# The first load of a residual add, issued as two half-loads from two queues

## The chip, the cores and the metric

The kernel runs on one core of one Trainium2 chip. The metric is the device time of one execution in microseconds; the time before is the median of three runs. Profiles come from a single profiled execution, so times inside the kernel are read against that execution and not against the median.

## The reference

```python
B, S, D = 512, 32, 640
x, fx: normal * 0.05, shape (512, 32, 640), bfloat16;  alpha: one bfloat16
def reference(x, fx, alpha):
    return x + alpha * fx
```

Each of x, fx and the output holds 10,485,760 bf16 values, 20.97 MB. The kernel must read two of them and write one: 62.92 MB in all, with one multiplication and one addition for each value.

## The kernel before, in words

All three tensors are seen as 128 partitions by 81,920 values, and a partition's row is counted in units of 512 values (1 KiB), of which it has 160. One SBUF tile `t` holds 207.5 units in each partition: units 0 to 160 are for x, and become the output in place; the rest is room for fx. Parts of fx that come late are put where x has not been loaded yet, or over fx parts that are used up.

The order of the work is written out by hand in the string `PLAN`, one step on a line, and the schedule is manual: each engine and queue gets its instructions in the order of the plan, and waits only where the data demand it. The steps are:

- `f a b p` loads units a to b of fx to place p of the tile (line 101, `load_f`). `x a b` loads x in place (line 97, `load_x`).
- `a` loads alpha (line 105), copied to 8 partitions of a small tile. DVE fills a row of ones (line 107), the matmul of line 109 spreads alpha over 128 partitions, and DVE copies it out of PSUM (line 111).
- `m a b` multiplies the fx part by alpha on DVE (line 114). `c a b` adds it to x on DVE (line 117).
- `s a b` stores units a to b (line 120). Of the three stores the first is held back until the multiplication of units 112.5 to 134.5 is done.

Every DMA of the kernel before is issued from SP (`nc.sync`): eleven large ones and the small one of alpha. Each large one has 128 rows, one a partition, of 8 to 64 KiB; consecutive rows lie 160 KiB apart in device memory. The plan begins:

```
f 0 8 95
a
f 8 65 103
x 0 64
x 64 95
f 65 112.5 160
m 0 8
m 8 65
c 0 8
```

The first step, `f 0 8 95`, is the smallest of the large loads: 128 rows of 8 KiB, 1 MiB in all. The first six loads wait for nothing; the later ones wait for DVE to have used the room that they overwrite. The ScalarE engine (ACT) has no work in this kernel. A completion counter stands behind every DMA; there are eight of them (DMAHW0 to DMAHW7 in the built program), given out in the order of issue, and a DMA that gets a used counter waits for the one that had it before. At the end a nop on SP (line 132) waits for all but the last store.

Of the kernel before, what the change touches and what calls it, by code (L numbers as in the profile page):

```python
# [1 line left out]

# [4 lines left out]

ALU = mybir.AluOpType
F32 = mybir.dt.float32

P = 128
K = 512
ROW = 160
SPARE = 47.5

LANES = 8

PLAN = """
f 0 8 95
a
f 8 65 103  # L30
x 0 64
# [5 lines that stand above are left out]
c 8 64  # L37
c 64 65
x 95 112.5
x 112.5 160  # L40
m 65 95
c 65 95
f 112.5 142.5 160
m 95 112.5
c 95 112.5
f 142.5 160 190
m 112.5 134.5
s 0 64 | m 112.5 134.5
m 134.5 142.5
c 112.5 142.5  # L50
m 142.5 160
c 142.5 160
s 64 128
s 128 160
"""


@with_exitstack
def kernel(
    ctx: ExitStack,  # L60
    tc: tile.TileContext,
    x: bass.AP,
    fx: bass.AP,
    alpha: bass.AP,
    out: bass.AP,
):
    nc = tc.nc
    xv, fv, ov = (
        t.flatten_outer_dims().rearrange("(p n) d -> p (n d)", p=P) for t in (x, fx, out)
    )  # L70
    assert xv.shape[1] == ROW * K

    consts = ctx.enter_context(tc.tile_pool(name="consts", bufs=1))
    psum = ctx.enter_context(tc.tile_pool(name="psum", bufs=1, space=bass.MemoryType.PSUM))
    flat = ctx.enter_context(tc.tile_pool(name="flat", bufs=1))
    ctx.enter_context(tc.manual_schedule())
    t = flat.tile([P, int((ROW + SPARE) * K)], x.dtype, name="t")
    info = mybir.DependencyInfo(mybir.DependencyClass.Sync, mybir.DependencyReason.DATA)

    lanes = {}  # L80
    lies = []
    done = []

    def at(a, b):
        return t[:, int(a * K) : int(b * K)]

    def of(v, a, b):
        return v[:, int(a * K) : int(b * K)]

    def place(a, b):  # L90
        for c, d, p in reversed(lies):
            if c <= a and b <= d:
                return at(p + a - c, p + b - c)
        raise ValueError(f"fx {a} to {b} lies nowhere in one piece")

    def load_x(a, b):
        done.append(nc.sync.dma_start(out=at(a, b), in_=of(xv, a, b)))

    def load_f(a, b, p):
        lies.append((a, b, p))  # L100
        done.append(nc.sync.dma_start(out=at(p, p + b - a), in_=of(fv, a, b)))  # L101

    def load_alpha():
        a_n = consts.tile([LANES, 1], alpha.dtype, name="a_n")
        done.append(nc.sync.dma_start(out=a_n[:], in_=alpha[None, :].to_broadcast([LANES, 1])))  # L105
        ones = consts.tile([1, P], alpha.dtype, name="ones")
        nc.vector.memset(ones[:], 1.0)  # L107
        a_ps = psum.tile([P, 1], F32, name="a_ps")
        done.append(nc.tensor.matmul(a_ps[:], ones[:], a_n[0:1, :], start=True, stop=True))  # L109
        lanes["a"] = consts.tile([P, 1], F32, name="a_f")  # L110
        nc.vector.tensor_copy(out=lanes["a"][:], in_=a_ps[:])  # L111

    def multiply(a, b):
        done.append(nc.vector.tensor_scalar_mul(place(a, b), place(a, b), lanes["a"][:]))  # L114

    def add(a, b):
        done.append(nc.vector.tensor_add(at(a, b), at(a, b), place(a, b)))  # L117

    def store(a, b):
        done.append(nc.sync.dma_start(out=of(ov, a, b), in_=at(a, b)))  # L120

    does = {"x": load_x, "f": load_f, "a": load_alpha, "m": multiply, "c": add, "s": store}
    begun = {}
    for step in filter(None, PLAN.split("\n")):
        step, *later = step.split(" | ")
        what, *numbers = step.split()
        does[what](*map(float, numbers))
        begun[step] = done[-1]
        for other in later:
            tc.add_manual_dep(done[-1].ins, begun[other].ins.name, info, reason="begins late")  # L130

    rest = nc.sync.nop(nofuse=True)
    for i in done[:-1]:
        tc.add_manual_dep(rest.ins, i.ins.name, info, reason="all but the last store")


# [1 line left out]
_INS = ['x', 'fx', 'alpha']  # L138
_OUTS = [((512, 32, 640), 'bfloat16')]


# [23 lines left out]
```

## Time and profile before

| | |
|---|---|
| median of 3 runs | 151.05 us (151.03 to 151.10) |
| profiled execution | 151.06 us |
| span in that execution, first to last instruction | 149.3 us |
| VectorE (DVE) busy | 66.5 us, 45% of the span, 16 instructions |
| DMA queue q1 | 1744 packets, 62.92 MB, 98.1% of 16 engines' span |
| mean rate over the span | 421 GB/s |

The span is what the views of the profile cover; 151.06 us less 149.3 us leaves some 1.8 us that lie around it. DMA engines, of which the core has 16, are shown by their mean busy share and by the rate of what they moved. In the table of stretches the bytes of a packet are credited to one moment, so a short stretch can show more than the engines can move, and its neighbour less. "Issue to landing" is the time from the instruction that issues a DMA to its completion. DVE is VectorE, PE is TensorE, SPq is the queue of SyncE.

### The profile page before, as it was taken

To read this page: it belongs to the slowest core of one execution; us is meant where nothing else is said; L and a number is where in the kernel's file an instruction comes from. 1 tells how busy PE (TensorE), PEld (TensorE's weight loads), DVE (VectorE), ACT (ScalarE), POOL (GpSimd) and SP (SyncE) were. 2 spreads that over 40 slices of the span, in tenths; PEclk is the share of its full clock that TensorE was granted. 3 is DMA by queue.
4 is the path that set the end of the run, shared out by engine and by line. 5 is a ranking of instruction groups with operands and counts; after the bars stand their busy time and mean duration, and the time that the engine had idled before them with its cause. 6 is when DMAs were issued, how large, how long until landed. Compare 5 with 4: busy or idle time off the path is not lost.

```text
span 149.3 us, 85 instructions
## 1 busy us (share of the span) xinstructions
PE 0.2 (0%) x1; PEld 0.1 (0%) x1; DVE 66.5 (45%) x16; POOL 0.2 (0%) x4
## 2 busy tenths in 40 slices
PE   0000000000000000000000000000000000000000
PEld 0000000000000000000000000000000000000000
DVE  0300008920069999029999900599997000000000
POOL 0000000000000000000000000000000000000000
DMA  5969998969699999999999799899896969697994
GB/s 149 617 266 500 500 461 351 562 281 562 281 408 442 447 417 443 456 388 565 430 417 417 340 461 461 379 516 457 386 562 281 562 281 562 281 562 334 430 439 202
DMA packets 1745, 62.92 MB, mean 421 GB/s; under 512 B 209, under 2 KB 209, under 8 KB 209
## 3 DMA queue, kind: packets, MB, share of 16 engines
q1 hardware_dynamic: 1744, 62.92, 98.1%
q14 instruction: 1, 0.00, 0.0%
HBM read 41.94 MB, written 20.97 MB: 421 GB/s over the span
## 4 chain that ended last, share of the span: by engine, by line
DMA 38%; DVE 31%; another core or an unknown queue 4%; issue 2%; SPq 1%; DVEq 0%
DMA t<-in_x_dram 27%; DVE t L117 26%; DMA t<-in_fx_dram 11%; DVE t L114 5%; SPq L101 0%; SPq L105 0%; DVEq L117 0%
## 5 line engine op out<-in xcount | busy, mean ns | idle before, releaser
L117 DVE TENSOR_TENSOR t<-t 128x15360 bf16<-128x15360 bf16 (+4 forms) x7 | 43.6, 6251 | 11.7 <-DMA t<-in_x_dram 11.6
L114 DVE TENSOR_SCALAR t<-t,a_f 128x4096 bf16<-128x4096 bf16 (+4 forms) x7 | 22.8, 3265 | 30.7 <-DMA t<-in_fx_dram 30.7
L111 DVE COPY a_f<-a_ps 128x1 f32<-128x1 f32 x1 | 0.2, 158 | 5.0 <-PE a_ps L109 5.0
L107 DVE MEMSET ones<- 1x128 bf16 x1 | 0.2, 165 | 0.8 <-PEq L149 0.8
L109 PE MATMUL a_ps<-a_n,ones 1*128 1x1 bf16 x1 | 0.2, 158 | 5.8 <-DMA a_n<-in_alpha_dram 5.8
L149 POOL MEMSET const-bfloat16-1.0<- 128x1 bf16 x1 | 0.1, 101 | 0.0
L149 POOL MEMSET const-uint8-127<- 128x1 uint8 x1 | 0.1, 101 | 0.0
L109 PEld LDWEIGHTS <-ones 1*128 1x128 bf16 x1 | 0.1, 99 | 1.0 <-DVE ones L107 1.0
L149 POOL MEMSET const-float32-0.0<- 128x1 f32 x1 | 0.1, 98 | 0.2 <-issue 0.2
L149 POOL MEMSET const-float32-1.0<- 128x1 f32 x1 | 0.1, 98 | 0.0
## 6 DMA issues: line engine op xcount, KB each, us to landing
t<-in_fx_dram SPq DMA_DIRECT2D x1, 7296.0 KB, 21.3
t<-in_fx_dram SPq DMA_DIRECT2D x1, 6080.0 KB, 63.0
t<-in_x_dram SPq DMA_DIRECT2D x1, 6080.0 KB, 25.7
out_dram<-t SPq DMA_DIRECT2D x1, 4096.0 KB, 33.7
t<-in_x_dram SPq DMA_DIRECT2D x1, 3968.0 KB, 49.2
t<-in_fx_dram SPq DMA_DIRECT2D x1, 3840.0 KB, 16.4
t<-in_x_dram SPq DMA_DIRECT2D x1, 2240.0 KB, 11.7
t<-in_fx_dram SPq DMA_DIRECT2D x1, 2240.0 KB
```

What stands on the lines that cost most here:

```text
L107: nc.vector.memset(ones[:], 1.0)
L109: done.append(nc.tensor.matmul(a_ps[:], ones[:], a_n[0:1, :], start=True, stop=True))
L111: nc.vector.tensor_copy(out=lanes["a"][:], in_=a_ps[:])
L114: done.append(nc.vector.tensor_scalar_mul(place(a, b), place(a, b), lanes["a"][:]))
L117: done.append(nc.vector.tensor_add(at(a, b), at(a, b), place(a, b)))
L149: nc = _bacc.Bacc("TRN2", target_bir_lowering=False, num_devices=1)
```

## The change

The step `f 0 8 95` becomes `g 0 8 95`. A new function issues the same load as two DMAs: partitions 0 to 63 from SP, as before the first thing in its queue, and partitions 64 to 127 from ACT. Both halves have 64 rows of 8 KiB with the same source and destination addresses as before. The other steps, their order and their queues are untouched.

```diff
 PLAN = """
-f 0 8 95
+g 0 8 95
 a
 f 8 65 103
...
+    def load_f_halves(a, b, p):
+        lies.append((a, b, p))
+        for queue, rows in ((nc.sync, slice(0, P // 2)), (nc.scalar, slice(P // 2, P))):
+            done.append(queue.dma_start(out=at(p, p + b - a)[rows, :], in_=of(fv, a, b)[rows, :]))
+
...
-    does = {"x": load_x, "f": load_f, "a": load_alpha, "m": multiply, "c": add, "s": store}
+    does = {"x": load_x, "f": load_f, "g": load_f_halves, "a": load_alpha, "m": multiply, "c": add, "s": store}
```

In the built program the instructions of PE, DVE and GpSimd (POOL) stay as they were, SP issues as many DMAs as before, and ACT issues one. Since there is one DMA more, each completion counter from alpha's on moves up by one place.

## The prediction

> **What bounds the kernel now.** I read the page's totals first, then the table of stretches, then the timelines of SP and DVE, then the DMA issues. A change of 0.2%, 0.3 us, is about the least that a measurement of this kernel can tell from none.
>
> The totals, from the page:
>
> ```profile
> PE 0.2 (0%) x1; PEld 0.1 (0%) x1; DVE 66.5 (45%) x16; POOL 0.2 (0%) x4
> q1 hardware_dynamic: 1744, 62.92, 98.1%
> ```
>
> DVE is busy for 45% of the span, the 16 DMA engines for 98.1% of theirs. Whether the missing 2% lie in gaps or at the ends is told by the table of stretches (DVE's busy time fourth, DMA share and GB/s last):
>
> ```profile
> 0.00:1.70 1.70, 0.00 (x0) 0.10 (x1) 0.17 (x1) 0.20 (x4) 1.00 0.00 0
> 1.70:2.10 0.40, 0.00 (x0) 0.00 (x0) 0.00 (x0) 0.00 (x0) 1.00 2.14 348
> 2.10:2.70 0.60, 0.00 (x0) 0.00 (x0) 0.00 (x0) 0.00 (x0) 1.00 0.43 109
> 2.70:3.30 0.60, 0.00 (x0) 0.00 (x0) 0.00 (x0) 0.00 (x0) 1.00 0.87 300
> 3.30:4.70 1.40, 0.00 (x0) 0.00 (x0) 0.00 (x0) 0.00 (x0) 1.00 1.01 421
> ...
> 100.00:120.00 20.00, 0.00 (x0) 0.00 (x0) 14.74 (x3) 0.00 (x0) 1.00 0.97 419
> 120.00:140.00 20.00, 0.00 (x0) 0.00 (x0) 0.00 (x0) 0.00 (x0) 1.00 0.97 419
> 140.00:147.50 7.50, 0.00 (x0) 0.00 (x0) 0.00 (x0) 0.00 (x0) 1.00 0.97 419
> 147.50:149.30 1.80, 0.00 (x0) 0.00 (x0) 0.00 (x0) 0.00 (x0) 1.00 0.01 0
> ```
>
> Nothing moves before 1.70 us, the rate is poor until 3.30 us, and from there to 147.5 us the engines are full. The page's issues give the full rate and the size of the poor beginning:
>
> ```profile
> t<-in_fx_dram SPq DMA_DIRECT2D x1, 7296.0 KB, 21.3
> t<-in_fx_dram SPq DMA_DIRECT2D x1, 1024.0 KB, 5.0
> t<-in_x_dram SPq DMA_DIRECT2D x1, 40.3
> ```
>
> The timeline of SP says when these three were issued, and the one of DVE who waits for them:
>
> ```profile
> 0.73 0.38 SPq L101 DMA_DIRECT2D t<-in_fx_dram  x1
> 1.16 0.35 SPq L105 DMA_DIRECT2D a_n<-in_alpha_dram  x1
> 1.57 0.35 SPq L101 DMA_DIRECT2D t<-in_fx_dram  x1
> 1.96 1.04 SPq L97 DMA_DIRECT2D t<-in_x_dram  x2
> ...
> 6.15 1.29 DVE L114 TENSOR_SCALAR t<-t,a_f 128x4096 bf16<-128x4096 bf16 x1
> 22.93 7.82 DVE L114 TENSOR_SCALAR t<-t,a_f 128x29184 bf16<-128x29184 bf16 x1 [15.49 <-DMA t<-in_fx_dram]
> 42.34 17.63 DVE L117 TENSOR_TENSOR t<-t 128x4096 bf16<-128x4096 bf16 x3 [11.60 <-DMA t<-in_x_dram]
> ```
>
> The load of fx 0 to 8 lands at 0.73 + 5.0 = 5.7 us, fx 8 to 65 at 1.57 + 21.3 = 22.9, x 0 to 64 (128 rows of 64 KiB, 8.39 MB) at 1.96 + 40.3 = 42.3. The last took 19.4 us behind the one before, so full rate is 8.39 MB / 19.4 us = 432 GB/s, and 62.92 MB take 145.6 us of it. The 8320 KB up to 22.9 us are 8.52 MB, 19.7 us, so the full-rate line starts at 3.2 us. Of these, 1.7 us lie before the first byte and about 0.4 us between a load's last byte (under 5.4 us for the first) and its landing (5.7): some 1.0 us of engine time is lost while the transfers get going.
>
> So the kernel is one gapless stream of DMA. What happens in the first 5 us passes to the end one for one, either way, since no gap later could swallow it, and the later issues hang on loads landing and shift with them.
>
> **The change part by part.**
>
> *SP's issue.* It issues a half where it issued the whole, at 0.73 us. The issue of 8 partitions took 0.35 us (line 105), of 128 took 0.38 and 0.35, so 64 rows save at most 0.03 us: 0. The queue behind (alpha, fx 8 to 65, x) keeps its times.
>
> *ACT's issue.* ACT leaves the barrier of the start at 0.7 us, SP at 0.6 (instructions of line 149):
>
> ```profile
> L149 SPq EVENT_SEMAPHORE  x1: 17/17/17, 0.6 to 0.6; - x1
> L149 ACTq EVENT_SEMAPHORE  x1: 17/17/17, 0.7 to 0.7; - x1
> ```
>
> ACT has nothing else in this kernel and nothing queued behind the issue. No row shows it issuing a DMA; between SP's fastest and slowest, 0.33 and 0.57 us (lines 101 and 97), I take SP's 0.38, so its half is out by about 1.2 us against SP's 1.1. Lateness itself is free, as SP's queue fills the engines meanwhile. What comes first into the engines cannot be earlier than SP's own first row, so no start is gained: 0.
>
> *The extra DMA's bookkeeping.* 209 packets under 512 B for 12 DMAs are some 17 each. The last stretch, 0.01 of 16 engines for 1.8 us, is 0.29 us for one store's small packets, or 0.02 us an engine: +0.02 us.
>
> *DVE's wait.* `m 0 8` waits for two loads and alpha instead of one load and alpha. It ran at 6.15 to 7.44, the next multiplication at 22.93, so 15.5 us of idle time cover it. Uncovered, the cost would be 1.29 us in front of the multiplication at 22.93, which ends at 30.75, again 11.6 us before anything needs it (42.34): 0.
>
> *The counters.* From alpha on each counter moves one place. The load of x 95 to 112.5 now has to wait for both halves of the first load, the fx load after it for the one that landed at 66.1, the stores for loads of 22.9, 42.3, 51.6 and 85.8 us. All are over when the issues come (59.7, 78.5, 98.1 and 107 us): 0.
>
> *How the rows run.* This is the open term. Every large DMA of the trace writes all 128 partitions, and at 432 GB/s a set of 64 takes 216. No row shows more into 64 partitions. Now 16 engines first get rows of partitions 0 to 63, and some 0.1 us later rows of 64 to 127 from a second queue. If the engines alternate out of step, both sets are written all the time: 0 us. If they go in step, one set is written while the other waits: the 1 MiB (1.05 MB) takes 4.9 us instead of 2.4, +2.4 us. In the poor beginning the engines wait anyway, and doubling the write time costs nothing. The bytes begun in 1.70 to 3.30 us are 0.4 x 348 + 0.6 x 109 + 0.6 x 300 = 385 KB of the 1049; the other 664 KB take 1.5 us at full rate and so cost 0 to 1.5 us more. Which engines clash is left to chance, but the kernel ends with the slowest of the 16, so I take half: +0.8 us.
>
> The Trainium skill (page "SBUF — State Buffer", section "Door 1: The DMA port swizzle") says that DMA bandwidth goes by how many of 16 ports the partitions reach, and that bit 6 of the partition number picks one of a pair, so that 0 to 63 reach 8 of them. By it one half alone would run at half rate, the upper of my two ends; no row here shows a half.
>
> The sum is 0 + 0 + 0.02 + 0 + 0 + 0.8 = +0.8 us, on the profiled execution 151.06 + 0.8 = 151.9 us, and 151.85 on the median of 151.05, which differs from it by 0.01.
>
> **The rivals.**
>
> *The stream is the same, only shuffled: 151.07 us.* The engines could write into 64 partitions as fast as into 128, or the two queues mix well enough. For it: every engine gets the same bytes, and the DMA share is flat in row sizes from 8 to 64 KiB. Against it: that flatness was only ever seen with 128 partitions. The cost is the 0.02 us of bookkeeping.
>
> The Trainium skill (page "DMA: Bandwidth & Descriptors", section "Rules for kernel authors") says of two transfers to disjoint partition halves not to bother, since both spread over the same 16 engines. By that rule it is this rival that comes.
>
> *The beginning gets better: 150.55 us.* The 1.0 us of lost engine time between 1.7 and 3.3 us could come from each engine having to wait on its first rows out of one queue. With two queues each engine has a row of the other half to go on with. For it: at 2.10 to 2.70 us the rate is 109 GB/s although SP has issued three more DMAs by 2.4 us, so something other than lack of work holds it. Against it: if that is device memory or the path to it, a second queue asks the same of it. All of it saved gives 150.05; half, 150.55. It decides on this side once more than the clash costs is saved.
>
> *ACT is so late that its rows mix with 57 KiB ones.* A row of 8 KiB then waits for a 57 KiB row of SP's queue each time: 7296 KB at 432 GB/s in 128 rows over 16 engines is 2.2 us a row, and four such waits land the half by some 9 us later, at 15 us. DVE has until 22.93 - 1.29 = 21.6 us. The stream is full throughout, so the time is 151.07 unless rows of one half clash with the long rows, which is the forecast's cost again.
>
> **How the numbers follow.** The clash that costs over 0.3 us: 0.62. The stream shuffled at no cost, with the late ACT: 0.18. The better beginning: 0.20, of which little lies beyond half a microsecond saved. The forecast's own range is 151.4 to 152.6 (0.3 to 1.5 us); the full clash, without the cover of the beginning, 153.5. The 8-in-10 range goes down to the better beginning's 150.55 and up to 153.0, which leaves out about one in ten above and one in twenty below. By sign: faster 0.20, same 0.18, slower 0.62.
>
> **What would show it.** A second queue in the table of queues with 64 large packets, 0.5 MB. ACT's issue at 0.7 to 0.8 us. Rates in 1.7 to 6 us: by the forecast well under 421 GB/s between 3.3 and 5 us, and fx 8 to 65 landing at 23.7 instead of 22.9; by the rivals at 22.9, or at 22.4. From there on all distances between landings as before (19.4 us to x 0 to 64), DVE's groups unchanged, and the span longer by just what the landing at 22.9 moved. I am wrong if the landing moves by less than 0.3 us or forward, and wrong in the whole picture if the difference arises after 23 us, or outside the span.

## The result and the profile after

| | before | after |
|---|---|---|
| median | 151.04 us (150.98 to 151.10, 4 runs) | 153.56 us (153.47 to 153.72, 4 runs) |
| profiled execution | 151.06 us | 153.47 us |
| span | 149.3 us | 151.7 us |

The ratio is 1.0164, with a 95% interval of 1.0152 to 1.0176: 2.5 us slower, not the 0.8 us forecast, and above the range's 153.0. The kernel does the same work with one more queue. From the page after:

```profile
PE 0.2 (0%) x1; PEld 0.1 (0%) x1; DVE 66.5 (44%) x16; POOL 0.2 (0%) x4
q1 hardware_dynamic: 1680, 62.39, 96.3%
q10 hardware_dynamic: 80, 0.52, 1.6%
```

DVE's busy time is the 66.5 us of before. The second queue, q10, carries ACT's 64 rows and their 16 small packets, 0.52 MB. The first stretches after, with the bounds of the table before as far as 4.70 us (DMA share and GB/s last):

```profile
1.70:2.10 0.40, 0.00 (x0) 0.00 (x0) 0.00 (x0) 0.00 (x0) 1.00 0.59 82
2.10:2.70 0.60, 0.00 (x0) 0.00 (x0) 0.00 (x0) 0.00 (x0) 1.00 1.00 164
2.70:3.30 0.60, 0.00 (x0) 0.00 (x0) 0.00 (x0) 0.00 (x0) 1.00 0.78 246
3.30:4.70 1.40, 0.00 (x0) 0.00 (x0) 0.00 (x0) 0.00 (x0) 1.00 1.04 240
4.70:5.40 0.70, 0.00 (x0) 0.00 (x0) 0.00 (x0) 0.00 (x0) 1.00 1.11 281
5.40:6.50 1.10, 0.00 (x0) 0.00 (x0) 0.00 (x0) 0.00 (x0) 1.00 1.24 292
```

The last three rows hold the story: the engines are shown as busy (1.04 to 1.24), but move 240 to 292 GB/s, where the kernel before had 421 from 3.30 to 4.70 us and 440 from 5.40 to 22.50. So these engines have work, and are held up in it. The share alone does not show this; it has to be read beside the GB/s.

The timelines of SP, ACT and DVE, and two rows of the DMA issues:

```profile
0.72 0.54 SPq L107 DMA_DIRECT2D t<-in_fx_dram  x1
0.73 0.56 ACTq L107 DMA_DIRECT2D t<-in_fx_dram  x1
1.31 0.51 SPq L111 DMA_DIRECT2D a_n<-in_alpha_dram  x1
...
25.35 7.82 DVE L120 TENSOR_SCALAR t<-t,a_f 128x29184 bf16<-128x29184 bf16 x1 [15.49 <-DMA t<-in_fx_dram]
44.77 17.63 DVE L123 TENSOR_TENSOR t<-t 128x4096 bf16<-128x4096 bf16 x3 [11.60 <-DMA t<-in_x_dram]
```

```profile
t<-in_fx_dram SPq DMA_DIRECT2D x1, 512.0 KB, 5.0
t<-in_fx_dram ACTq DMA_DIRECT2D x1, 512.0 KB, 7.6
```

SP's half lands at 0.72 + 5.0 = 5.7 us, a time at which the whole load had landed in the kernel before. ACT's was issued at the same time and lands at 8.3. DVE's multiplication of fx 8 to 65 starts at 25.35 instead of 22.93, and x 0 to 64 is added at 44.77 instead of 42.34. They moved by 2.42 and 2.43 us, and the span by 2.4. From 25 us on all distances are as before.

### The profile page after: what moved, and what is told of

Same layout as the page of the kernel before. It is cut to its first block, busy times and chain, and to the rows that moved or that the text cites. A ratio compares the mean times of both kernels' runs of the same rounds, so it can differ in the third digit from the quotient of the medians.

```text
span 151.7 us, 87 instructions
## 1 busy us (share of the span) xinstructions
PE 0.2 (0%) x1; PEld 0.1 (0%) x1; DVE 66.5 (44%) x16; POOL 0.2 (0%) x4
## 4 chain that ended last, share of the span: by engine, by line
DMA 39%; DVE 31%; another core or an unknown queue 4%; issue 2%; SPq 1%; DVEq 0%
DMA t<-in_x_dram 28%; DVE t L123 26%; DMA t<-in_fx_dram 11%; DVE t L120 5%; SPq L107 0%; SPq L111 0%; SPq L102 0%; DVEq L123 0%
```

## The experiments

Three theories for the 2.4 us:

- **Sides.** A transfer that writes only partitions 0 to 63, or only 64 to 127, goes at about half rate.
- **Queues.** Two queues on the same engines, or ACT's queue, are slow.
- **Start.** The loss belongs to the first rows of the stream, or to two issues at the same time.

All edits are to `load_f_halves`, in the loop over queues and rows, unless shown otherwise. A `+for` that stands alone replaces the first line of that loop. Besides the views, the trace has a record of each row of a DMA, with its queue, its start and the time it took; no view prints them, and where the text says "by the rows" it goes by these records. In the kernel before, a row of fx 8 to 65 (57 KiB) takes 2.15 us, and a row of the first load (8 KiB) that starts after 3.30 us takes 0.31.

**1. Both halves from SP.**

```diff
-for queue, rows in ((nc.sync, slice(0, P // 2)), (nc.scalar, slice(P // 2, P))):
+for queue, rows in ((nc.sync, slice(0, P // 2)), (nc.sync, slice(P // 2, P))):
```

> Both halves are issued from SP, one behind the other, and ACT issues nothing. By the partition theory (all 16 engines write into the same 64 partitions, which take about half of the 432 GB/s, and the halves run one after the other) the slow first 1 MiB stays: fx 8 to 65 lands near 25.0 us, time 153.2 us, that is 151.05 + 2.4 less what the start of two issues at once had cost (up to 0.3). By the queue theory (the loss comes from two queues being served by the same engines, or from ACT's queue) it is gone: fx 8 to 65 lands at 22.9, time 151.1 us. SP's issue takes 0.35 to 0.38 us again if the 0.54 us came from ACT issuing at the same time.

Measured: 153.07 us against 150.98, ratio 1.0135 (1.0120 to 1.0150). The loss stays without the second queue, which speaks against "queues". The row of the line that issues the halves:

```profile
L107 SPq DMA_DIRECT2D t<-in_fx_dram x2: 541/558/575, 0.7 to 1.3; - x2
```

The issue of a half takes 0.54 to 0.58 us with ACT silent. So SP's 0.54 us in the changed kernel needs no contest with ACT to explain it.

**2. Halves by columns.** All 128 partitions in both, 4 KiB rows.

```diff
+        h = (a + b) / 2
+        for queue, c, d in ((nc.sync, a, h), (nc.scalar, h, b)):
+            done.append(queue.dma_start(out=at(p + c - a, p + d - a), in_=of(fv, c, d)))
```

> The load is split by columns: units 0 to 4 of all 128 partitions from SP, units 4 to 8 from ACT, 256 rows of 4 KiB in place of 128 of 8 KiB. By the partition theory the rows run at full rate (about 155 ns each) and only the later start is left: 151.1 to 151.4 us. By the queue theory two queues are still served at once: 153.5 us, rows from the second queue as slow as in the changed kernel.

Measured: 150.96 us against 150.98, ratio 1.0001 (0.9991 to 1.0010). Two queues at the same time from the very start cost nothing. Nor do two issues at once:

```profile
L108 ACTq DMA_DIRECT2D t<-in_fx_dram x1: 398/398/398, 0.7 to 0.7; - x1
L108 SPq DMA_DIRECT2D t<-in_fx_dram x1: 386/386/386, 0.7 to 0.7; - x1
```

With 128 partitions each, both issues take the usual 0.39 to 0.40 us. "Queues" and "two issues at once" fall here.

**3. The whole load from ACT.**

```diff
+for queue, rows in ((nc.scalar, slice(0, P)),):
```

> The whole load, 128 rows, goes out from ACT in one DMA; SP begins with alpha and fx 8 to 65. By the partition theory nothing is slow but the start: 151.05 to 151.4 us. By the theory that ACT's queue is the slow one the 8 KiB rows take 600 ns and more: 153.5 us. If SP's 0.54 us of issue came from ACT issuing at the same time, SP's first issue (alpha) shows it here too.

Measured: 150.90 us, ratio 0.9995 (0.9986 to 1.0005). ACT's queue is as good as SP's. SP's queue being free earlier (fx 8 to 65 issued at 1.18 us instead of 1.57) brings nothing that can be measured.

**4. Another cut: 32 to 95, and the rest.**

```diff
+for queue, rows in ((nc.sync, slice(32, 96)), (nc.scalar, slice(0, 32)), (nc.scalar, slice(96, P))):
```

> The same number of partitions in SP's transfer, another set: 32 to 95 from SP, then 0 to 31 and 96 to 127 as two transfers from ACT. If it is the number of partitions in a transfer that halves the rate, all of it is slow: 153.5 us or more. If it is which partitions (0 to 63 share one set of ways in, 64 to 127 another), SP's 64 rows run at about 310 ns and only ACT's rows at 620: half of the 2.4 us, with the later start 152.3 to 152.6 us. By the queue theory 153.5 us, and SP's and ACT's rows alike.

Measured: 152.19 us against 150.98, ratio 1.0076 (1.0061 to 1.0091), 1.2 us more: about half the loss, as "sides" has it. But the stretches show no clean fast and slow part (304 GB/s from 3.30 to 4.70 us), since the three pieces were in flight together. It needed a longer load.

**5 and 6. Half of the load left out.** Partitions 0 to 63 alone, or 32 to 95 alone, with GpSimd filling the rest with zeros.

> Leaves out half of the first load: only partitions 0 to 63 of fx 0 to 8 are loaded, from SP; GpSimd fills the other half with zeros, beside everything else. 512 KB less are moved, 1.2 us of full rate. By the partition theory (rows of 0 to 63 share one half of the ways in) the 512 KB take as long as the whole 1 MiB did at full rate, so nothing is saved: 151.0 to 151.3 us. By the theory that the two halves disturb each other, half of the load alone is fast: 149.8 to 150.1 us.

> The same with the other set of 64: only partitions 32 to 95 of fx 0 to 8 are loaded, from SP; GpSimd fills 0 to 31 and 96 to 127. If it matters which partitions (both sides of 64 are reached), the half runs at full rate and 1.2 us are saved less the later start of a 64-row issue: 149.9 to 150.2 us. If any transfer of 64 partitions is slow, it is as half_low: 151.0 to 151.3 us.

Measured: 150.84 to 152.80 us for the lower half, and 150.40 to 152.83 for the middle, both over ten runs. The spread within one kernel is larger than what the two were to tell apart, so nothing is concluded from these times. The saving of 1.2 us that was expected for the middle does not show in them. Where the spread comes from was not looked into. The landing of the half itself is clearer, in one profiled execution of each, first the lower half, then the middle:

```profile
t<-in_fx_dram SPq DMA_DIRECT2D x1, 512.0 KB, 4.9
```
```profile
t<-in_fx_dram SPq DMA_DIRECT2D x1, 512.0 KB, 3.7
```

Partitions 0 to 63 alone take 4.9 us from issue to landing, about as long as the whole load before (5.0), and 32 to 95 take 1.2 us less, as "sides" has it.

**7 and 8. The second load in halves.** The first is whole again; fx 8 to 65 (rows of 57 KiB, 7.47 MB) takes the cut, once all from SP and once from SP and ACT.

```diff
-g 0 8 95
+f 0 8 95
 a
-f 8 65 103
+g 8 65 103
```

> The first load is whole again; the second, fx 8 to 65 with rows of 57 KiB, goes out in halves 0 to 63 and 64 to 127, both from SP. By the partition theory its 7.47 MB run at half rate, rows of 4.3 us in place of 2.15, 17.3 us more: 168 us. If the loss was one of starting up (first rows of a stream, 8 KiB rows) it is not larger than before: 151 to 153.5 us.

> As big_sp, but the upper half of fx 8 to 65 goes out from ACT. If an engine takes rows of the two queues in turn, out of step with its neighbours, both sides are written at once and most of the 17.3 us is not paid: 151 to 160 us. If the engines go in step, or take one queue's rows after the other's, 168 us as big_sp.

Measured: 170.97 us from SP (ratio 1.1317, 1.1282 to 1.1353) and 170.18 from both queues (1.1267, 1.1229 to 1.1305). The loss grew from 2 to 20 us with a load 7.1 times as large, so it does not belong to the start. The stretch from 10 to 40 us, in the kernel before, with both halves from SP, and with SP and ACT:

```profile
10.00:40.00 30.00, 0.00 (x0) 0.00 (x0) 7.82 (x1) 0.00 (x0) 1.00 1.00 435
```
```profile
10.00:40.00 30.00, 0.00 (x0) 0.00 (x0) 0.00 (x0) 0.00 (x0) 1.00 0.93 191
```
```profile
10.00:40.00 30.00, 0.16 (x1) 0.00 (x0) 1.44 (x2) 0.00 (x0) 1.00 0.91 187
```

435 GB/s against 191 and 187, with the engines busy for nine tenths of the time or more. When the pieces landed, from SP, and from SP and ACT:

```profile
DMA to landing us min/median/max: 23.1/32.1/41.1
```
```profile
DMA to landing us min/median/max: 37.2/39.0/40.8
```

From SP the halves are issued at 1.6 and 2.1 us and land at 24.7 and 43.2, one after the other: 18.5 us for 3.74 MB, 202 GB/s. From two queues they land at 37.9 (ACT) and 42.4 (SP), and it helped by less than 1 us.

A stretch credits a row of 57 KiB to one moment, so 187 and 191 GB/s are rough. By the rows, the median row takes 4.57 us from SP and 4.56 from the two queues, against 2.15 before: 16 engines with a row each then move 204 GB/s instead of 434. Summed and divided by the 16 engines, the rows of fx 8 to 65 take 18.7 us more in the kernel from SP than before, and the 64 KiB rows of x, the next behind them, 0.9 us more. With two queues, rows of both were in flight together for only about 9 of the 30 us, eight engines on each from 14.5 to 17.5 and from 28 to 31 us; the rows begun in those stretches took 4.54 to 4.58 us all the same. Halves that wrote to both sides at once did not do so at any better rate. Why not is not shown.

**9. The long load with the cut at 32 and 96**, all from SP. This and the next one, and 12 and 13, have the plan of 7 and 8.

```diff
+for queue, rows in ((nc.sync, slice(32, 96)), (nc.sync, slice(0, 32)), (nc.sync, slice(96, P))):
```

> fx 8 to 65 in three pieces, all from SP: partitions 32 to 95, then 0 to 31, then 96 to 127. If it matters which partitions a transfer holds, the 64 rows of the first piece run at full rate (3.74 MB in 8.6 us, some 420 GB/s from 5.4 to 14 us) and only the two outer pieces at the 187 GB/s of the halves: half of the 20 us, 161 us. If any transfer of less than 128 partitions is slow, 187 GB/s from the start and 171 us.

Measured: 162.60 us against 150.85, ratio 1.0773 (1.0741 to 1.0805). The row of the issues, and two stretches:

```profile
DMA to landing us min/median/max: 15.4/23.6/32.0
```
```profile
5.40:14.00 8.60, 0.16 (x1) 0.00 (x0) 1.45 (x2) 0.00 (x0) 1.00 0.83 339
17.00:31.00 14.00, 0.00 (x0) 0.00 (x0) 0.00 (x0) 0.00 (x0) 1.00 0.96 200
```

The first piece, 32 to 95, lands at 1.6 + 15.4 = 17.0 us, where the lower half of the same size had landed at 24.7. The outer pieces run at 200 GB/s. So 64 partitions are not slow as such. The stretch of the piece has only 339 GB/s instead of some 430, but by the rows that is not its own rate: the third 16 of its 64 rows take 2.15 us (median), as in the kernel before. Its first 32 rows, behind the first load, take 2.15 to 3.55 us, and its last ones run into the slow outer rows.

**10. The long load as even and odd partitions**, both from SP.

```diff
+for queue, rows in ((nc.sync, slice(0, P, 2)), (nc.sync, slice(1, P, 2))):
```

> fx 8 to 65 as two pieces from SP: the 64 even partitions, then the 64 odd ones. Each piece reaches both sides of partition 64. If only the side matters (0 to 63 against 64 to 127), both run at full rate: 151 us. If finer groups of partitions matter and the 16 engines take consecutive rows of the piece, two engines fall on one group here as well: 187 GB/s and 171 us.

Measured: 152.53 us against 150.85, ratio 1.0106 (1.0077 to 1.0136). These are two transfers of 64 rows, as in experiment 7, with nothing different but which partitions they hold, and 18 of the 20 us are gone. Its stretch from 10 to 40 us, and when the pieces, issued at 1.6 and 2.2 us, landed:

```profile
10.00:40.00 30.00, 0.00 (x0) 0.00 (x0) 7.82 (x1) 0.00 (x0) 1.00 1.02 444
```
```profile
DMA to landing us min/median/max: 14.1/18.2/22.2
```

The rate is 444 GB/s. The pieces land at 15.7 and 24.4 us: 8.7 us for the 3.74 MB of the second piece, 429 GB/s. What is left, 1.7 us, lies before that: the stretch from 6 to 10 us has 321 GB/s. By the rows, the first 32 of the first piece, right behind the first load, take 2.15 to 3.43 us, and from the third 16 on the median is 2.15. Why the first ones are slow is open.

**11. The changed kernel with even and odd partitions**, from SP and ACT.

```diff
-for queue, rows in ((nc.sync, slice(0, P // 2)), (nc.scalar, slice(P // 2, P))):
+for queue, rows in ((nc.sync, slice(0, P, 2)), (nc.scalar, slice(1, P, 2))):
```

> The changed kernel with another choice of halves: the 64 even partitions from SP, the 64 odd ones from ACT. Two queues, 64 rows each, as in the changed kernel; each half reaches both sides of partition 64. If the side is what costs, the 2 us of slow rows go, and the later start of a 64-row issue (0.3 us) and the clash of neighbours where one row order follows another (1.6 us with 57 KiB rows, less with 8 KiB ones) stay: 151.2 to 152.0 us. If two queues with 64 rows each are enough to be slow, 153.5 us.

Measured: 151.24 us against 150.95, ratio 1.0018 (1.0006 to 1.0029). This is the change itself, two queues and 64 rows each, but for the partitions in a half: 0.3 us instead of 2.5.

```profile
1.70:2.10 0.40, 0.00 (x0) 0.00 (x0) 0.00 (x0) 0.00 (x0) 1.00 0.61 123
...
3.30:4.70 1.40, 0.00 (x0) 0.00 (x0) 0.00 (x0) 0.00 (x0) 1.00 0.94 392
...
22.90 7.82 DVE L120 TENSOR_SCALAR t<-t,a_f 128x29184 bf16<-128x29184 bf16 x1 [15.59 <-DMA t<-in_fx_dram]
```

From 3.30 us on it moves 392 GB/s, where the changed kernel moves 240. The slow start up to 2.10 us (123 against the 348 of before) is still there, but it costs nothing by the time fx 8 to 65 lands: its multiplication starts at 22.90 us, before the change at 22.93. In the profiled execution the 0.3 us arises only after 42.35 us, where x 0 to 64 is still on time (42.34 before), and by 66.29 us (66.07 before). Where it comes from was not looked into.

**12 and 13. Which end of the transfer.** All the cuts above split the partitions of the tile and the rows in device memory alike. These two halve only one of them and take even and odd rows of the other, with the long load, both pieces from SP. Another row of fx than the reference's is then added in that range. The first has halves in the tile and even and odd rows in device memory, the second the opposite.

```diff
+for rows, source in ((slice(0, 64), slice(0, P, 2)), (slice(64, P), slice(1, P, 2))):
+    done.append(nc.sync.dma_start(out=at(p, p + b - a)[rows, :], in_=of(fv, a, b)[source, :]))
...
+for rows, source in ((slice(0, P, 2), slice(0, 64)), (slice(1, P, 2), slice(64, P))):
```

> Every cut so far split the tile's partitions and the rows in device memory alike. Here fx 8 to 65 goes to partitions 0 to 63 from the even rows in device memory, and to 64 to 127 from the odd rows, both from SP; so another row of fx is multiplied and added in that range than the reference has. If the side of the tile is what costs, 171 us and some 190 GB/s from 10 to 40 us. If reading one half of the tensor in device memory is what costs, 152.5 us and 435 to 444 GB/s.

> The counterpart: the even partitions of the tile are filled from the lower 64 rows in device memory, the odd partitions from the upper 64, both from SP; again another row of fx is added in that range than the reference has. If the side of the tile costs, 152.5 us; if the half of device memory costs, 171 us.

Measured: 170.74 us with the tile halved (ratio 1.1304, 1.1262 to 1.1346) and 152.31 us with device memory halved (1.0091, 1.0065 to 1.0116), both against 151.01. The stretch from 10 to 40 us, in the one and in the other:

```profile
10.00:40.00 30.00, 0.00 (x0) 0.00 (x0) 0.00 (x0) 0.00 (x0) 1.00 0.93 195
```
```profile
10.00:40.00 30.00, 0.00 (x0) 0.00 (x0) 7.82 (x1) 0.00 (x0) 1.00 1.01 435
```

The loss goes with the tile's partitions. Halving device memory adds nothing: 152.31 us against the 152.53 of experiment 10. So the cause is which partitions of the tile a transfer writes. By what way the side of partition 64 holds the engines up, no run shows.

No version beat the kernel before: the best two, the whole load from ACT and the halves by columns, cannot be told from it.

## Why the prediction was wrong

**The bound was right.** The kernel is one gapless stream of DMA, and what the first load lost came out at the end one for one: 2.42 us at 22.93, 2.43 at 42.34, 2.4 in the span. It does not hold to a tenth: with columns the landings came 0.2 us early (22.71 and 42.17), and at 66.03 us (66.07 before) nothing of that was left.

**The step that failed is "How the rows run".** Its cause held, that writing one side at a time is slow; its size did not. It took half of 1.5 us, and the rows of the first load lost 1.5 us. Two things around it were put at nothing. By the rows, 2.3 of the 2.42 us are:

- *The rows of the first load: 1.45 us.* The sum of their times, divided by the 16 engines, is 4.67 us instead of 3.22. This is the term that the prediction put at 0.8, and it comes out at its upper end, 1.5.
- *The rows behind them: 0.53 us.* The first 16 rows of fx 8 to 65 took 2.42 to 2.90 us instead of 2.15. The sum had no term for them. Both halves from SP, and 32 to 95 with the rest from ACT, show the same in theirs (2.40 to 2.89 and 2.35 to 2.85 us). Why rows of all 128 partitions are slow in that place is open.
- *The first byte: 0.31 us.* The first row starts at 2.04 us instead of 1.74.

Experiment 1 has nearly all of it with one queue (2.1 us). Two choices lay behind the main term, and only the first was wrong.

- *The half for engines that alternate out of step.* They neither alternated nor went in step. SP's half landed at 5.7 us and ACT's at 8.3, and by the rows ACT's first one starts at 4.07 us, while SP's last ends at 4.99: the sides were written one after the other, although both were issued at the same time. Where rows of both queues were in flight together (experiment 8), they were no faster. The upper end, each half at half rate, was the value.
- *The cover of the slow beginning.* I let the first 385 KB run free. Without that the upper end would have been 2.4 us, and the rows lost 1.45, so it held about as taken. Only, by 3.30 us the changed kernel had moved less: 0.4 x 82 + 0.6 x 164 + 0.6 x 246 = 279 KB. So 94 rows instead of 81 were left for the time after, and they took 0.57 us each on average instead of 0.31.

The rule of the Trainium skill that I set beside this step (page "SBUF — State Buffer", section "Door 1: The DMA port swizzle") fits the cuts tried: rows with one value of bit 6 take 4.57 us, and rows of 32 to 95 and of the even partitions, which have both values, 2.15 us once they have settled. It gave the upper end, which I halved.

**"SP's issue: 0" was wrong by a little.** The issue of 64 partitions took 0.52 to 0.59 us wherever it occurs (0.54 in the changed kernel), the first issue of 128 partitions 0.37 to 0.40, with ACT issuing beside it or not. I had argued from 8 partitions (0.35) and 128 (0.38 and 0.35) to 64 between them. By the rows, the first row of the kernel starts at 2.04 to 2.13 us where all first transfers have 64 rows (experiments 1, 5, 6 and 11 and the changed kernel), and at 1.72 to 1.75 where they have 128. The 0.31 us need not be lost: experiment 11 starts as late, its rows of the first load take 2.92 us in the same sum instead of 3.22, and fx 8 to 65 is on time.

**The rest of the sum held.** ACT issued at 0.73 us, and nothing hung on it. `m 0 8` ran at 8.57 to 9.86 us, far ahead of the multiplication at 25.35, which waited the same 15.49 us as before. The moved counters cost nothing: after 25 us every distance is as it was.

**The rivals.** "The same stream, only shuffled" is what happens with columns, with the whole load from ACT and nearly with even and odd partitions, but not with halves at 64. The rule of the Trainium skill on two halves that I set beside it (page "DMA: Bandwidth & Descriptors", section "Rules for kernel authors") is right that they are not worth it and serialize. Sharing the engines, the reason it gives, does not by itself make the price of 2.5 us: the columns share the engines too. "The beginning gets better" came in no kernel's time. The late ACT did not come in the changed kernel.

## What to carry to other kernels

When a load is to be cut in two, cut it by columns, which cost nothing here, or by even and odd partitions (0.3 us, and 1.7 with the long rows), not at partition 64. A transfer that holds only one side ran at less than half rate (204 against 434 GB/s), and a second queue with the other side did not make up for it. Read the DMA share beside the GB/s: here a share of 1 with half the usual rate was a transfer that was held up, not one that was missing. Where a row has never been seen and the end of the kernel waits for the slowest of many equal engines, take the upper end of the price rather than its middle.

## What the runs showed that was not expected

- One side of partition 64 is written at 204 GB/s, below even half of 432. Twice the time would have been 17.3 us more for the long load; it had 20 us.
- Rows of all 128 partitions right behind a one-sided transfer are slow too: the first 16 in the changed kernel took 2.42 to 2.90 us instead of 2.15.
- Issuing a DMA of 64 partitions takes longer (0.54 us) than one of 128 (0.38) or 8 (0.35), and the DMA issued behind it, alpha's, took 0.51 instead of 0.35.
- A short DMA can wait long behind long rows of another queue. With half of fx 8 to 65 issued from ACT at 0.73 us, alpha, issued from SP at 1.17, let DVE go on at 19.57 us instead of 5.96. It was covered: DVE then waited another 21.48 us for fx 8 to 65.
